# Attention with a relative bias, then a mixture of adapters: another order for the last outputs

## The chip, the core and the metric

The kernel runs on one core of one Trainium2 chip. The metric is the device time of one execution in microseconds (us). Before the change it is 201.61 us, the median of three runs (200.8 to 201.71).

A core has a matrix engine (TensorE, in the profile PE, with its weight loads as PEld), three others that compute (VectorE or DVE, ScalarE or ACT, GpSimd or POOL), and SyncE (SP), which here issues nearly all DMA transfers, among them all stores of the output. The engines run side by side, each takes its own instructions in the order of the program, and they wait for each other through semaphores. Matrix products land in PSUM, a small memory of eight banks, from which VectorE or ScalarE must copy them to SBUF before they can be stored or used as an operand.

## The reference

Two parts. The first is attention over 8 batches, 8 heads, 576 positions and 64 channels, with a bias that depends on the distance of the two positions only:

```python
    scores = scale * np.matmul(q, k.transpose(0, 1, 3, 2))
    ...
    bias = bias_table[bucket]
    scores = scores + bias.transpose(2, 0, 1)[None, :, :, :]
    scores = scores - np.max(scores, axis=-1, keepdims=True)
    attn = np.exp(scores)
    attn = attn / (np.sum(attn, axis=-1, keepdims=True) + 1e-09)
    return np.matmul(attn, v).astype(np.float32)
```

The heads of a position are then put side by side, which gives x with 4608 rows of 512. The second part picks for each row the two of eight experts with the largest logits, and adds their low-rank products (rank 16), weighted by a softmax over the two:

```python
    logits = x @ w_gate
    topk = np.argpartition(-logits, K, axis=1)[:, :K]
    ...
            z = x[mask] @ A[e]
            delta[mask] += w[mask, k, None] * (z @ B[e])
    return (x + delta).astype(np.float32)
```

## The kernel before

**Units.** One unit is a batch and a pair of heads; there are 32, U0 and U1 are the last two. The first 512 positions of a batch are its main part, the last 64 its tail. `keys` makes scores of a unit on TensorE (product, then a bias product into the same bank) and ScalarE takes their exp. `values` multiplies the exps with v, with the sums of the softmax in an extra column, and `normalise` on VectorE takes the reciprocal of the sums (L557) and multiplies (L558); the result goes to the tile `xs` of the batch. In the last two units the scores are made in halves of the queries: `keys_half(u, j, m)` makes one score tile for query half j, with its exp at L451. The values of half j need both m.

**Rows of the second part.** The output of a batch has four main tiles of 128 rows, (b, 0) to (b, 3); the tails of two batches make one tile (b, 4) with odd b. Tiles 0 and 1 need half j = 0 of all four units of the batch, tiles 2 and 3 need half 1. L is the last batch, 7. Each tile goes through these steps: x is turned (`turn` with `x_item`: transposes on TensorE, L368 and L370, and a copy from PSUM, L372), a product with A and the gate weights gives 128 low-rank values and 8 logits (`moe_z` or `zsum`), the gate is worked out (`moe_s` on GpSimd, `moe_w` with a tanh on ScalarE and the rest on GpSimd, because a softmax over two is a tanh of half the difference), the gated values zt are turned, and a last product with B gives the delta. Then x is added and the tile stored.

There are two ways to the output. `moe_d` and `out_dve` make the product with B and let VectorE add x while it leaves PSUM (L303). `out_x` adds x on TensorE, as four products of the turned x with the identity (`x_first`, L832) ahead of the product with B (L838), and the result is copied out by ScalarE or VectorE (L840). A store is one DMA of 256 KB, for a tail tile two of 128 KB (L331).

**PSUM.** Two banks rotate for values and small things (`mp`, through `bank()` at the end). The other six are three pairs that rotate for scores and for turned tiles: `score_tile` gives the next pair, and whoever asks waits until the pair's last reader is done. For the last outputs the three pairs are given back and become six single banks, `fin(i, k)`: pair i, counted from the pair whose turn it is, bank k.

**The order of the work** is the order of the program text, engine by engine. The end before: scores of U0 (1,1) and U1 (1,0); the turn of zt of (L-1,0) and (L-1,1); gating of (L-1,2) and (L-1,3); values of U1 half 0; `moe_d` of (L-1,0); scores of U1 (1,1); one turn for zt of (L-1,2), (L-1,3) and x of (L,0), (L,1); then U0 half 1 with `moe_d` of (L-1,1) ahead of it; low-rank values of (L,0), (L,1), with their gate on GpSimd; a turn for the tail tile and most of x of (L,2), (L,3). Then the values of U1 half 1 in two pieces, with the outputs of (L-1,2), (L-1,3) and products of the last tiles between them. From them comes `xl`, the last quarter of x of (L,2) and (L,3); it is turned to xb, which completes z1, the low-rank values and logits of these two tiles. Their gate is worked out straight from PSUM: the two largest by L959, their negated sum `ns`, tanh on ScalarE (`fth`, L963), the mask and the gate on VectorE, and `fzt`. The outputs follow in the order (L,0), (L,2), (L,3), (L,4), (L,1).

Of the kernel before, what the change touches and what calls it, by code (L numbers as in the profile page):

```python
# [38 lines left out]
def kernel(  # L39
# [11 lines left out]
    nc = tc.nc  # L51
# [299 lines left out]
            t.group, t.k = g, k  # L351
        return g

    def turn(items):
        n = sum(it[1] for it in items)
        assert n <= 16
        ps = score_tile("tx", (128, 2, 1024), BF16)
        sb = txp.tile([128, 16, 2, 64], BF16, name="tx", tag="tx")
        s0 = 0
        for _, k, src, quarter in items:  # L360
            for i in range(k):
                c = s0 + i
                for a in range(2):
                    rows = slice(a * 64, a * 64 + 64)
                    cols = slice(c * 64, c * 64 + 64)
                    if quarter:
                        for h in range(2):
                            nc.tensor.transpose(ps[h * 64:h * 64 + 64, a, cols], src(i, a, h), ident[rows, rows])  # L368
                    else:
                        nc.tensor.transpose(ps[:, a, cols], src(i, a), ident[rows, rows])  # L370
            s0 += k
        nc.vector.tensor_copy(sb[:, :n], ps.rearrange("p a (c i) -> p c a i", i=64)[:, :n])  # L372
        s0 = 0
        for done, k, *_ in items:
            done(sb, s0)
            s0 += k
# [17 lines left out]
    def x_item(t, g0=0, g1=HP):  # L394
        if g0 == 0:
            t.xT = [None] * HP

        def done(sb, s0):
            for hp in range(g0, g1):
                t.xT[hp] = sb[:, s0 + hp - g0].rearrange("p a i -> p (a i)")  # L400
        return done, g1 - g0, lambda i, *a: t.src(g0 + i, *a), t.quarter

    def zt_item(t):
        def done(sb, s0):
            t.zT = sb[:, s0].rearrange("p a i -> p (a i)")
        zt, k = t.group.zt, t.k
        return done, 1, lambda i, a: zt[a * 64:a * 64 + 64, k].rearrange("p e r -> p (e r)"), False
# [182 lines left out]
    def moe_w(g):  # L590
        n = g.n
        sm, mk = g.gating
        th = ms.tile([128, n, E], FP32, name="th", tag=f"th{n}")
        nc.scalar.activation(th, sm, ACT.Tanh)
        g0 = ms.tile([128, n, E], FP32, name="g0", tag=f"g0{n}")
        nc.gpsimd.tensor_tensor(g0, th, mk, op=ALU.mult)
# [3 lines left out]
        nc.gpsimd.tensor_tensor(g.zt, g.z[:, :, :ER].rearrange("p n (e r) -> p n e r", e=E),  # L600
                                gate.to_broadcast((128, n, E, r)), op=ALU.mult)
# [247 lines left out]
    def bank():  # L849
        return mp.tile([128, 512], FP32, name="fm", tag="mm")  # L850
# [31 lines left out]
    halves_of(U0, (1, 0))  # L882
    step(U0, 0, [(L - 2, 4)], z=(L - 1, 3))
    halves_of(U0, (1, 1))
    halves_of(U1, (1, 0))
    turn([zt_item(T(L - 1, 0)), zt_item(T(L - 1, 1))])
    moe_w(groups[(L - 1, 2)])

    pv = bank()
    pv_main(U1, pv, 0, KO)  # L890
# [1 line left out]
    for h in range(2):  # L892
# [5 lines left out]
                            _ap(rc, 0, [[1, 4], [0, D]]), op=ALU.mult)  # L898
    nc.vector.tensor_tensor(_ap(xs[b], hp * 320 + 256, [[HP * 320, 2], [1, D]]),
                            _ap(pv, 260, [[W1, 2], [1, D]]), _ap(rc, 4, [[1, 2], [0, D]]), op=ALU.mult)  # L900
# [12 lines left out]
    fps = [ctx.enter_context(tc.tile_pool(name=f"fin{i}_ps", bufs=1, space=bass.MemoryType.PSUM))  # L913
# [14 lines left out]
    pv_last(U1, pv, 1)  # L928
    nc.vector.reciprocal(rc[:, 6:], _ap(pv, D, [[W1, 4]]))
    xl = ms.tile([128, 2, 128], BF16, name="xl", tag="xl")  # L930
    nc.vector.tensor_tensor(xl.rearrange("p f (h d) -> p (f h) d", h=2), _ap(pv, 0, [[W1, 4], [1, D]]),
                            _ap(rc, 6, [[1, 4], [0, D]]), op=ALU.mult)
    moe_w(groups[(L, 0)])
    gx = groups[(L, 4)]
    act(gx.z[:, 0, :], zx[:, :136])
    nc.vector.max(gx.top[:, 0, :], gx.z[:, 0, ER:])
    moe_s(gx)

    def full_turn(n, ps, src, copy, tag):
        v = ps[:, :64 * n].bitcast(BF16).rearrange("p (n t) -> p n t", n=n)  # L940
# [3 lines left out]
        copy(t, v)  # L944
# [6 lines left out]
    g = groups[(L, 2)]  # L951
    n = 2
    zl = z1[:, :136 * n].rearrange("p (n e) -> p n e", n=n)
    ns = ms.tile([128, n, 1], FP32, name="fns", tag="fns")
    mk = ms.tile([128, n, E], FP32, name="fmk", tag="fmk")
    th = ms.tile([128, n, E], FP32, name="fth", tag="fth")
    gate = ms.tile([128, n, E], FP32, name="fgate", tag="fgate")
    for i in range(n):
        nc.vector.max(g.top[:, i, :], zl[:, i, ER:])  # L959
    nc.vector.scalar_tensor_tensor(out=ns, in0=g.top[:, :, 0:1], scalar=-1.0, in1=g.top[:, :, 1:2],  # L960
                                   op0=ALU.mult, op1=ALU.subtract)
    for i in range(n):
        nc.scalar.activation(th[:, i, :], zl[:, i, ER:], ACT.Tanh, scale=2.0, bias=ns[:, i, :])  # L963
    nc.vector.tensor_tensor(mk, zl[:, :, ER:], g.top[:, :, 1:2].to_broadcast((128, n, E)), op=ALU.is_ge)  # L964
    moe_w(gx)
    j0 = groups[(L, 0)]
    zt0 = full_turn(2, bank(), lambda i: j0.zt[:, i].rearrange("p e r -> p (e r)"), dve, "zt0")
    for i in range(2):
        T(L, i).zT = zt0[:, i, :]
    nc.vector.scalar_tensor_tensor(out=gate, in0=th, scalar=1.0, in1=mk, op0=ALU.add, op1=ALU.mult)  # L970
    g.zt = ms.tile([128, n, E, r], BF16, name="fzt", tag="fzt")
    nc.vector.scalar_tensor_tensor(out=g.zt, in0=zl[:, :, :ER].rearrange("p n (e r) -> p n e r", e=E),
                                   scalar=0.5, in1=gate.to_broadcast((128, n, E, r)),
                                   op0=ALU.mult, op1=ALU.mult)
    out_x(T(L, 0), fin(0, 0))
    d3 = fin(2, 1)
    x_first(T(L, 2), d3)
    d4 = fin(1, 0)
    x_first(T(L, 3), d4)
    zt1 = full_turn(2, bank(), lambda i: g.zt[:, i].rearrange("p e r -> p (e r)"), dve, "zt1")  # L980
    for i in range(2):
        T(L, 2 + i).zT = zt1[:, i, :]
    out_x(T(L, 2), d3, False)
    out_x(T(L, 3), d4, False, dve)
    zt2 = full_turn(1, bank(), lambda i: gx.zt[:, i].rearrange("p e r -> p (e r)"), dve, "zt2")
    T(L, 4).zT = zt2[:, 0, :]
    out_x(T(L, 4), fin(1, 1))
    out_dve(T(L, 1), fin(0, 1))


# [28 lines left out]
```

## Time and profile before

| what | value |
|---|---|
| runs before | 201.61, 201.71, 200.8 us |
| profiled execution | 200.68 us, its span 198.8 us |
| granted TensorE clock, mean of the span | 0.949 |
| PE busy | 178.5 us (90%) |
| ACT busy | 162.8 us (82%) |
| DVE busy | 134.8 us (68%) |
| POOL busy | 122.6 us (62%) |

The span goes from the first to the last instruction of the profiled execution. In a page the line of an engine's tenths cuts the span in 40 slices of 4.97 us; a 9 is 90% busy or more. A row of the timeline gives the start and the length in us, the engine, the line of the kernel and the operation, the tile it writes and the tiles it reads, sizes and how many were merged; in brackets the engine's idle time before it and what ended that. SPq is SyncE's queue of DMA issues: the length there is that of the issuing, merged rows include the gaps, and the transfer comes later. A row of groups gives the busy time of all of a kind in us and the mean of one in ns. A row of the table of windows gives a stretch and its length, the busy time of PE, PEld, DVE, ACT and POOL with the number of instructions, the granted TensorE clock, the busy share of the 16 DMA engines and what they moved in GB/s.

### The profile page before, as it was taken

How to read it: one execution, taken by the hardware profiler on the slowest of the kernel's cores; microseconds unless marked ns; L12 is line 12 of the kernel's file. 1: busy time of each engine (PE TensorE's matmuls, PEld its weight loads, DVE VectorE, ACT ScalarE, POOL GpSimd, SP SyncE). 2: the span in 40 equal slices, each digit the busy share in tenths (PEclk: the TensorE clock that was granted, in tenths of full speed). 3: DMA queues.
4: the chain of work that ended last, by engine and by line, in shares of the span. 5: the costliest groups of instructions: out<-in, count | busy, mean ns of one | idle time of the engine just before them, and what ended most of it. 6: DMA issues, size and time to landing. Idle time of an engine off the chain costs nothing. (4 is left out here: it accounts for less than half of the span.)

```text
span 198.8 us, 9936 instructions
## 1 busy us (share of the span) xinstructions
PE 178.5 (90%) x4262; PEld 129.4 (65%) x4262; DVE 134.8 (68%) x340; ACT 162.8 (82%) x204; POOL 122.6 (62%) x299
## 2 busy tenths in 40 slices
PE   7498998988999999999999999999999999996750
PEld 2254676666777677777777777776777777884620
DVE  6544464564577778778877687778776786797541
ACT  3457779986999899999999999999999999984230
POOL 5633556495777759495949594959494939253420
PEclk9755599999999999999999999999999999999996
DMA  5767978978889978998798878759897911123416
GB/s 135 234 167 215 292 183 212 242 173 254 244 211 261 268 190 236 297 270 219 196 288 264 203 227 274 217 169 217 233 284 230 297 69 56 62 72 93 162 73 190
DMA packets 68484, 40.65 MB, mean 204 GB/s; under 512 B 22217, under 2 KB 63705, under 8 KB 68441
## 3 DMA queue, kind: packets, MB, share of 16 engines
q1 hardware_dynamic: 67896, 39.76, 70.5%
q8 instruction: 33, 0.54, 1.2%
q10 hardware_dynamic: 544, 0.26, 0.4%
q14 instruction: 11, 0.08, 0.2%
HBM read 30.56 MB, written 9.45 MB: 201 GB/s over the span
## 5 line engine op out<-in xcount | busy, mean ns | idle before, releaser
L431 ACT ACTIVATE pk<-sc 128x1024 bf16<-128x1024 f32 x120 | 113.8, 1034 | 6.0 <-PE sc L427 6.0
L422 PE MATMUL sc<-tx 64*64 64x512 bf16 x480 | 50.7, 401 | 0.0
L518 PEld LDWEIGHTS <-pk 128*128 128x128 bf16 x1024 | 38.1, 98 | 9.1 <-issue 2.1
L427 PE MATMUL sc<-Wt,anti 64*64 64x256 bf16 (+1 forms) x480 | 43.6, 318 | 0.2
L518 PE MATMUL pv<-v,pk 128*128 128x65 bf16 x992 | 42.2, 194 | 1.2 <-DVE xn L558 0.7
L372 DVE COPY tx<-tx 128x2048 bf16<-128x2048 bf16 (+6 forms) x36 | 36.3, 1009 | 10.3 <-PE tx L370 8.3
L494 ACT ACTIVATE pt<-sc 128x1024 bf16<-128x1024 f32 x32 | 32.8, 1025 | 7.8 <-PE sc L492 6.0
L558 DVE TENSOR_TENSOR xn<-pv,rc 128x320 bf16<-128x320 f32 x62 | 30.5, 491 | 2.1
L581 POOL TENSOR_TENSOR a<-z,top 128x16 f32<-128x16 f32 (+2 forms) x16 | 3.6, 224 | 37.0 <-DVE top L571 33.5
L557 DVE RECIPROCAL rc<-pv 128x5 f32<-128x5 f32 x62 | 11.9, 192 | 20.8 <-PE pv L565 11.2
L303 DVE TENSOR_TENSOR ot<-dl,xn 128x512 f32<-128x512 f32 x26 | 17.9, 689 | 11.3 <-PE dl L614 10.8
L422 PEld LDWEIGHTS <-tx 64*64 64x64 bf16 x480 | 16.6, 108 | 10.0 <-issue 1.2
L136 POOL CAST v<-vs 128x512 bf16<-128x512 f32 x32 | 20.3, 634 | 3.6 <-DMA vs<-in_v_dram 3.1
L140 POOL CAST qn<-qs 128x512 bf16<-128x512 f32 x29 | 17.7, 612 | 5.6 <-DMA qs<-in_q_dram 5.3
L427 PEld LDWEIGHTS <-anti 64*64 64x64 bf16 x480 | 18.8, 109 | 1.1 <-issue 1.0
L140 POOL CAST kn<-ks 128x512 bf16<-128x512 f32 x29 | 17.8, 614 | 1.1 <-DMA ks<-in_k_dram 1.1
L499 POOL TENSOR_TENSOR pt<-pt,EL 128x128 bf16<-128x128 bf16 x32 | 13.8, 430 | 7.0 <-DVE EL L233 6.0
L535 PE MATMUL pv<-v,pt 128*128 128x65 bf16 x248 | 17.8, 195 | 0.0
L526 PE MATMUL pv<-vb,pt 128*128 128x130 bf16 x124 | 17.6, 225 | 0.0
L370 PEld LDWEIGHTS <-qn 64*128 64x128 bf16 x256 | 7.6, 96 | 12.5 <-issue 6.4
L535 PEld LDWEIGHTS <-pt 128*128 128x128 bf16 x256 | 14.2, 99 | 0.0
L565 PE MATMUL pv<-AW,tx 128*128 128x136 bf16 x124 | 12.5, 224 | 0.0
(141 smaller groups left out, 299.6 us busy)
## 6 DMA issues: line engine op xcount, KB each, us to landing
qs<-in_q_dram SPq DMA_DIRECT2D x32, 256.0 KB, 4.4
vs<-in_v_dram SPq DMA_DIRECT2D x64, 128.0 KB, 4.2
out_dram<-ot SPq DMA_DIRECT2D x32, 256.0 KB, 3.6
ks<-in_k_dram SPq DMA_DIRECT2D x62, 128.0 KB, 4.4
vt<-in_v_dram SPq DMA_DIRECT2D x16, 128.0 KB, 4.2
out_dram<-ot SPq DMA_DIRECT2D x8, 128.0 KB, 2.7
qkt<-in_q_dram SPq DMA_DIRECT2D x7, 128.0 KB, 4.6
qkt<-in_k_dram SPq DMA_DIRECT2D x7, 128.0 KB, 4.3
```

Of the source, the lines that this page charges most:

```text
L136: eng.tensor_copy(t[:, :, :, :D].rearrange("p c h d -> p h c d"), s)
L140: copy(t.rearrange("p c h d -> p h c d"), s)
L303: nc.vector.tensor_tensor(ot.rearrange("p (g x) -> p g x", g=HP), dl.rearrange("p (g x) -> p g x", g=HP), x[:, j, :, 2 * f:2 * f + 2, :].r ...
L372: nc.vector.tensor_copy(sb[:, :n], ps.rearrange("p a (c i) -> p c a i", i=64)[:, :n])
L422: nc.tensor.matmul(sc[prt, h, :], lhsT=kT[rows, c * 128 + f * 64:c * 128 + f * 64 + 64], rhs=qT[rows, :], start=True, stop=False, skip_gro ...
L427: nc.tensor.matmul(_ap(sc[prt, h, :], p0, [[256, 2], [128, 2], [1, n]]), lhsT=turned(h), rhs=_ap(Wt[rows, hp, :], 2 * y0 + (GP if e else 1 ...
L431: nc.scalar.activation(probs[u][0][:, c, :, :], sc, ACT.Exp, scale=scale)
L494: nc.scalar.activation(probs[u][1][:, 64:], sc.rearrange("p h x -> p (h x)"), ACT.Exp, scale=scale)
L518: nc.tensor.matmul(pv[:, o:o + W1], lhsT=pk_slice(u, c, h, j + 2 * f), rhs=vm[:, c, h, :], start=first, stop=False, skip_group_check=True)
L526: nc.tensor.matmul(_ap(pv, h * W1, [[130, 2], [1, W1]]), lhsT=probs[u][1][:, x0:x0 + 128], rhs=tvs[b % 2][:, 2 * hp + h].rearrange("p f d ...
L535: nc.tensor.matmul(pv[:, o:o + W1], lhsT=probs[u][1][:, x0:x0 + 128], rhs=vts[u % NV][:, c, h, :], start=False, stop=False, skip_group_che ...
L558: nc.vector.tensor_tensor(xs[b][:, j, hp], _ap(pv, 0, [[W1, 5], [1, D]]), _ap(rc, 6 * j, [[1, 5], [0, D]]), op=ALU.mult)
```

## The change

Only the end of the program is changed, from the scores of the last unit on.

- The last score tile, U1 (1,1), is made directly behind U1 (1,0).
- `moe_d` of (L-1,0) and (L-1,1) go from between the values to the end, and (L-1,2), (L-1,3) too. The values of U1 half 0, U0 half 1 and U1 half 1 follow each other, with only turns of x between them; the values of U1 half 1 are one piece.
- `turn` takes the copying engine as an argument. The turn of x of (L,0), (L,1) and that of the tail tile are now separate and ScalarE copies them; the zt of (L-1,2), (L-1,3) are turned in the end, by `full_turn`.
- The group (L,0), (L,1) gets the gate straight from PSUM that (L,2), (L,3) had, each with a bank and tiles of its own. The gate is split in three functions, `gate_top`, `gate_tanh` and `gate_sum`, so that the two groups interleave. The tail tile keeps its gate on GpSimd.
- All nine last outputs go by `out_x`, six copied by ScalarE and three by VectorE; for most, `x_first` is put ahead of the time at which zt is turned, in a bank of its own.

```diff
-    def turn(items):
+    def turn(items, copy=nc.vector.tensor_copy):
...
-        nc.vector.tensor_copy(sb[:, :n], ps.rearrange("p a (c i) -> p c a i", i=64)[:, :n])
+        copy(sb[:, :n], ps.rearrange("p a (c i) -> p c a i", i=64)[:, :n])
...
     halves_of(U0, (1, 1))
-    halves_of(U1, (1, 0))
+    halves_of(U1, (1, 0), (1, 1))
     turn([zt_item(T(L - 1, 0)), zt_item(T(L - 1, 1))])
-    moe_w(groups[(L - 1, 2)])
...
-    moe_d(T(L - 1, 0))
-
-    halves_of(U1, (1, 1))
-    turn([zt_item(T(L - 1, 2)), zt_item(T(L - 1, 3)), x_item(T(L, 0)), x_item(T(L, 1))])
-    step(U0, 1, [(L - 1, 1)])
-    zj = bank()
-    for i in range(2):
-        zsum(zj, i, T(L, i), range(HP), i == 0)
-    zcopy(groups[(L, 0)], zj, dve)
-    turn([x_item(T(L, 4)), x_item(T(L, 2), 0, 3), x_item(T(L, 3), 0, 3)])
...
+    step(U0, 1)
+    moe_w(groups[(L - 1, 2)])
+    turn([x_item(T(L, 0)), x_item(T(L, 1))], act)
 
     pv = bank()
-    pv_main(U1, pv, 1, (0, 2))
-    out_x(T(L - 1, 2), fin(1, 0))
-    out_x(T(L - 1, 3), fin(1, 1))
-    z1, zx = fin(2, 0), fin(2, 1)
-    zsum(zx, 0, T(L, 4), range(HP), True)
-    for i in range(2):
-        zsum(z1, i, T(L, 2 + i), range(HP - 1), i == 0)
-    pv_main(U1, pv, 1, (1, 3), False)
+    pv_main(U1, pv, 1, KO)
     pv_last(U1, pv, 1)
...
-    moe_w(groups[(L, 0)])
-    gx = groups[(L, 4)]
-    act(gx.z[:, 0, :], zx[:, :136])
-    nc.vector.max(gx.top[:, 0, :], gx.z[:, 0, ER:])
-    moe_s(gx)
+    turn([x_item(T(L, 4))], act)
+    turn([x_item(T(L, 2), 0, 3), x_item(T(L, 3), 0, 3)])
...
+    def turned_gate(zt, n, ids, copy, tag):
+        t = full_turn(n, bank(), lambda i: zt[:, i].rearrange("p e r -> p (e r)"), copy, tag)
+        for i, x in enumerate(ids):
+            T(*x).zT = t[:, i, :]
+
+    z0, z1 = fin(0, 0), fin(0, 1)
+    for i in range(2):
+        zsum(z0, i, T(L, i), range(HP), i == 0)
     xb = full_turn(2, bank(), lambda f: xl[:, f, :], dve, "xb")
+    zx = bank()
+    zsum(zx, 0, T(L, 4), range(HP), True)
+    for i in range(2):
+        zsum(z1, i, T(L, 2 + i), range(HP - 1), i == 0)
     for i in range(2):
         T(L, 2 + i).xT[HP - 1] = xb[:, i, :]
         zsum(z1, i, T(L, 2 + i), range(HP - 1, HP), False)
...
+    gx = groups[(L, 4)]
+    act(gx.z[:, 0, :], zx[:, :136])
+    nc.vector.max(gx.top[:, 0, :], gx.z[:, 0, ER:])
+    moe_s(gx)
...
+    def gate_top(i, zl):
+        w = Gate()
+        w.g, w.zl = groups[(L, i)], zl[:, :272].rearrange("p (n e) -> p n e", n=2)
+        w.ns = ms.tile([128, 2, 1], FP32, name="fns", tag=f"fns{i}")
+        w.th = ms.tile([128, 2, E], FP32, name="fth", tag=f"fth{i}")
+        for k in range(2):
+            nc.vector.max(w.g.top[:, k, :], w.zl[:, k, ER:])
+        nc.vector.scalar_tensor_tensor(out=w.ns, in0=w.g.top[:, :, 0:1], scalar=-1.0, in1=w.g.top[:, :, 1:2],
+                                       op0=ALU.mult, op1=ALU.subtract)
+        return w
+
+    def gate_tanh(w):
+        for k in range(2):
+            nc.scalar.activation(w.th[:, k, :], w.zl[:, k, ER:], ACT.Tanh, scale=2.0, bias=w.ns[:, k, :])
+
+    def gate_sum(w, i):
...
+        nc.vector.tensor_tensor(mk, w.zl[:, :, ER:], w.g.top[:, :, 1:2].to_broadcast((128, 2, E)), op=ALU.is_ge)
+        nc.vector.scalar_tensor_tensor(out=gate, in0=w.th, scalar=1.0, in1=mk, op0=ALU.add, op1=ALU.mult)
+        w.g.zt = ms.tile([128, 2, E, r], BF16, name="fzt", tag=f"fzt{i}")
+        nc.vector.scalar_tensor_tensor(out=w.g.zt, in0=w.zl[:, :, :ER].rearrange("p n (e r) -> p n e r", e=E),
+                                       scalar=0.5, in1=gate.to_broadcast((128, 2, E, r)),
+                                       op0=ALU.mult, op1=ALU.mult)
+
+    w0 = gate_top(0, z0)
+    gate_tanh(w0)
+    w1 = gate_top(2, z1)
+    gate_tanh(w1)
     moe_w(gx)
...
+    out_x(T(L - 1, 0), fin(1, 0))
+    gate_sum(w0, 0)
+    p1 = fin(1, 1)
+    x_first(T(L - 1, 1), p1)
+    d = [fin(2, 0), fin(2, 1)]
     for i in range(2):
...
+        x_first(T(L, i), d[i])
+    turned_gate(w0.g.zt, 2, ((L, 0), (L, 1)), act, "zt0")
+    gate_sum(w1, 2)
+    turned_gate(groups[(L - 1, 2)].zt, 2, ((L - 1, 2), (L - 1, 3)), act, "zta")
+    out_x(T(L - 1, 1), p1, False)
     for i in range(2):
...
+        d.append(fin(1 - i, 0))
+        x_first(T(L, 2 + i), d[-1])
+    out_x(T(L, 0), d[0], False)
+    turned_gate(gx.zt, 1, ((L, 4),), dve, "zt2")
+    turned_gate(w1.g.zt, 2, ((L, 2), (L, 3)), dve, "zt1")
+    out_x(T(L, 1), d[1], False, dve)
+    out_x(T(L - 1, 2), fin(1, 1))
+    out_x(T(L, 2), d[2], False)
+    out_x(T(L, 3), d[3], False, dve)
+    out_x(T(L, 4), fin(0, 1), True, dve)
+    out_x(T(L - 1, 3), fin(2, 0))
```

More of the change, by code (lines that the diff above doesn't have):

```diff
@@ L900 @@
                             _ap(pv, 260, [[W1, 2], [1, D]]), _ap(rc, 4, [[1, 2], [0, D]]), op=ALU.mult)
-    moe_d(T(L - 1, 0))
-    halves_of(U1, (1, 1))
-    turn([zt_item(T(L - 1, 2)), zt_item(T(L - 1, 3)), x_item(T(L, 0)), x_item(T(L, 1))])
-    step(U0, 1, [(L - 1, 1)])
-    zj = bank()
-    for i in range(2):
-        zsum(zj, i, T(L, i), range(HP), i == 0)
-    zcopy(groups[(L, 0)], zj, dve)
-    turn([x_item(T(L, 4)), x_item(T(L, 2), 0, 3), x_item(T(L, 3), 0, 3)])
+    step(U0, 1)
+    moe_w(groups[(L - 1, 2)])
+    turn([x_item(T(L, 0)), x_item(T(L, 1))], act)
+    pv = bank()
+    pv_main(U1, pv, 1, KO)
+    pv_last(U1, pv, 1)
+    nc.vector.reciprocal(rc[:, 6:], _ap(pv, D, [[W1, 4]]))
+    xl = ms.tile([128, 2, 128], BF16, name="xl", tag="xl")
+    nc.vector.tensor_tensor(xl.rearrange("p f (h d) -> p (f h) d", h=2), _ap(pv, 0, [[W1, 4], [1, D]]),
+                            _ap(rc, 6, [[1, 4], [0, D]]), op=ALU.mult)
+    turn([x_item(T(L, 4))], act)
+    turn([x_item(T(L, 2), 0, 3), x_item(T(L, 3), 0, 3)])
     s0 = next(turns)
@@ L950 @@
         zsum(z1, i, T(L, 2 + i), range(HP - 1, HP), False)
[L951 to L961, printed above, removed]
@@ L962 @@
-    for i in range(n):
-        nc.scalar.activation(th[:, i, :], zl[:, i, ER:], ACT.Tanh, scale=2.0, bias=ns[:, i, :])
-    nc.vector.tensor_tensor(mk, zl[:, :, ER:], g.top[:, :, 1:2].to_broadcast((128, n, E)), op=ALU.is_ge)
-    moe_w(gx)
-    j0 = groups[(L, 0)]
-    zt0 = full_turn(2, bank(), lambda i: j0.zt[:, i].rearrange("p e r -> p (e r)"), dve, "zt0")
-    for i in range(2):
-        T(L, i).zT = zt0[:, i, :]
-    nc.vector.scalar_tensor_tensor(out=gate, in0=th, scalar=1.0, in1=mk, op0=ALU.add, op1=ALU.mult)
@@ L971 @@
[L971 to L980, printed above, removed]
@@ L981 @@
-    for i in range(2):
[L982 to L988, printed above, removed]
+    gx = groups[(L, 4)]
+    act(gx.z[:, 0, :], zx[:, :136])
+    nc.vector.max(gx.top[:, 0, :], gx.z[:, 0, ER:])
+    moe_s(gx)
+    class Gate:
+        pass
+    def gate_top(i, zl):
[8 more added lines that the diff above has]
+        return w
@@ new lines, in gate_tanh @@
+    def gate_tanh(w):
+        for k in range(2):
+            nc.scalar.activation(w.th[:, k, :], w.zl[:, k, ER:], ACT.Tanh, scale=2.0, bias=w.ns[:, k, :])
+    def gate_sum(w, i):
+        mk = ms.tile([128, 2, E], FP32, name="fmk", tag=f"fmk{i}")
+        gate = ms.tile([128, 2, E], FP32, name="fgate", tag=f"fgate{i}")
+        nc.vector.tensor_tensor(mk, w.zl[:, :, ER:], w.g.top[:, :, 1:2].to_broadcast((128, 2, E)), op=ALU.is_ge)
[4 more added lines that the diff above has]
+                                       op0=ALU.mult, op1=ALU.mult)
```

6 lines of the change are left out of this document (removed).

## The prediction

> **What bounds the kernel now.** I read the page first. TensorE and ScalarE are both nearly full up to the last four of the 40 slices (4.97 us each), in which they empty.
>
> ```profile
> span 198.8 us, 9936 instructions
> PE   7498998988999999999999999999999999996750
> ACT  3457779986999899999999999999999999984230
> ```
>
> So the end, from about 178 us on, has no full engine and is a chain. The chain of waits (from a start of about 190 us; start, length, what) says which:
>
> ```profile
> 191.32 0.30 DVE zt L944
> 191.67 0.62 PE f L838 x2
> ...
> 193.83 0.69 DVE ot L303
> ```
>
> Turn, project, evict: one output after another, the last eviction done at 194.52. Behind it stands SyncE's queue:
>
> ```profile
> 186.39 1.08 SPq L309 DMA_DIRECT2D out_dram<-ot  x2
> 191.42 0.33 SPq L309 DMA_DIRECT2D out_dram<-ot  x1
> 192.71 0.81 SPq L309 DMA_DIRECT2D out_dram<-ot  x2
> 194.23 1.11 SPq L331 DMA_DIRECT2D out_dram<-ot  x2
> 195.43 0.54 SPq L309 DMA_DIRECT2D out_dram<-ot  x1
> ```
>
> The two halves of the tail store hold it until 195.34, so the last store starts 0.91 us after its data. Then the transfers (table of windows; the last two columns are the busy share of the DMA engines and GB/s):
>
> ```profile
> 192.20:192.90 0.70, 0.35 (x6) 0.18 (x4) 0.59 (x1) 0.48 (x1) 0.00 (x0) 1.00 0.93 351
> 194.30:194.90 0.60, 0.00 (x0) 0.00 (x0) 0.22 (x1) 0.00 (x0) 0.00 (x0) 1.00 1.02 386
> 195.40:196.20 0.80, 0.00 (x0) 0.00 (x0) 0.00 (x0) 0.00 (x0) 0.00 (x0) 0.64 0.96 213
> 196.20:197.20 1.00, 0.00 (x0) 0.00 (x0) 0.00 (x0) 0.00 (x0) 0.00 (x0) 0.50 0.95 285
> 197.20:198.00 0.80, 0.00 (x0) 0.00 (x0) 0.00 (x0) 0.00 (x0) 0.00 (x0) 0.50 0.19 69
> ```
>
> The bytes end near 197.35 (0.19 of 0.8 us), 1.45 us before the span's end. Three readings for later. A 256 KB store fills the engines for 0.70 us (first row: 351 GB/s x 0.70 us is 246 of its 262 thousand bytes). The tail pair and the last store together (524 thousand bytes) take from 195.4 to 197.35, 1.95 us. And the bytes of a store begin some 0.8 us after its issue (the output issued at 191.42 fills the first row, from 192.2).
>
> **The front of the change.** Up to the scores of half (1,0) of the last unit, at 178.31, the programs agree. These rows set what follows:
>
> ```profile
> 178.00 1.94 ACT L451 ACTIVATE pk<-sc 128x1024 bf16<-128x1024 f32 x2 [0.34 <-PE sc L447]
> 178.24 0.11 PEld L370 LDWEIGHTS <-zt 64*128 64x128 bf16 x4
> 178.41 0.67 PE L518 MATMUL fm<-v,pk 128*128 128x65 bf16 x16
> 179.54 0.20 DVE L896 RECIPROCAL frc<-fm 128x6 f32<-128x6 f32 x1
> 180.11 0.28 DVE L899 TENSOR_TENSOR xn<-fm,frc 128x128 bf16<-128x128 f32 x1
> 180.49 1.02 ACT L451 ACTIVATE pk<-sc 128x1024 bf16<-128x1024 f32 x1 [0.15 <-PE sc L447]
> 181.75 0.12 PEld L370 LDWEIGHTS <-zt 64*128 64x128 bf16 x4 [1.51 <-POOL zt L600]
> 182.17 0.75 PEld L518 LDWEIGHTS <-pk 128*128 128x128 bf16 x16
> 187.36 0.42 DVE L931 TENSOR_TENSOR xl<-fm,frc 128x256 bf16<-128x256 f32 x1
> ```
>
> *Scores at once.* The scores of (1,1) follow directly, some 0.4 us of TensorE, and their exp joins the two before it: 179.94 to about 180.96 instead of 180.49 to 181.51. The price: three score buffers rotate, and the turn of the two gated tiles now takes the buffer that the exp ending near 178.97 must free, so it goes at 179.02 instead of 178.24. TensorE works in order; the values of U1 half 0 move from 178.41 to about 179.2, their reciprocal from 179.54 to 180.32, the last normalise (L899) to 181.17. Loss on the path: 0.8 us. This wait isn't in the old trace; its bounds are 0 (buffer already free) and 2.0 us (if it waited for the newest exp, 180.96, instead).
>
> *Values ahead.* The two moe_d and the turn with its 1.51 us wait for GpSimd no longer stand ahead of U0 half 1: its values start at about 180.15 instead of 182.17; with 1.13 us of values (as from 178.41 to 179.54) and 0.7 for a reciprocal and one product (three instructions take 0.85 from 179.54 to 180.39), this half is normalised near 182.0. The gating that was waited for (moe_w) now has until 186 us. The turn of tiles (L,0) and (L,1) comes at 181.2 to 181.6, then U1 half 1 runs in one piece from 181.55, since its exp is done by 181: without the tails 0.8 of those 1.13 us. With a reciprocal of 0.2 from 182.4 and 0.42 for xl, xl ends at about 183.0 instead of 187.78: 4.8 us earlier. That is the main gain; it comes from outputs, turns and a wait taken out from ahead of it.
>
> *Turned tiles on ScalarE.* Neither copy has a row. These stand nearest:
>
> ```profile
> L840 ACT COPY ot<-f 128x512 f32<-128x512 f32 x5 | 2.8, 587 | 6.7 <-DMA out_dram<-ot 4.3 <-PE f L838 1.6 <-ACT th L594 0.8
> L473 ACT ACTIVATE pcx<-cn 128x256 bf16<-128x256 f32 x1 | 0.4, 378 | 0.0
> L372 DVE COPY tx<-tx 128x1280 bf16<-128x1280 bf16 x2 | 1.6, 816 | 1.3 <-PE tx L370 1.3
> L944 DVE COPY zt<-fm 128x256 bf16<-128x256 bf16 x2 | 0.6, 286 | 0.5 <-PE fm L942 0.5
> ```
>
> The copy for (L,0), (L,1) has 1024 elements: I take 1.02 us, the exp of that size at 180.49; below, VectorE's 0.82 for 1280 elements; above, two 512-copies, 1.17. It runs 181.7 to 182.7, that of (L,4) (512 elements, 0.59) to 183.3. ScalarE is idle there in any case. VectorE meanwhile makes xl and the third turn's copy (to about 183.55) and xb (to 183.85).
>
> **The gates.** Before, xl's end at 187.78 led to the end of fzt at 190.82, 3.04 us:
>
> ```profile
> 187.70 0.16 DVE L936 MAX8 top<-z 128x8 f32<-128x8 f32 x1
> 188.91 0.25 DVE L959 MAX8 top<-f 128x8 f32<-128x8 f32 x2 [0.46 <-PE fm L942]
> 189.44 0.43 ACT L963 ACTIVATE fth<-f,fns 128x8 f32<-128x8 f32 x2 [2.32 <-DVE fns L960]
> 189.91 0.17 DVE L964 TENSOR_TENSOR fmk<-f,top 128x16 f32<-128x16 f32 x1 [0.56 <-ACT fth L963]
> 190.12 0.21 POOL L596 TENSOR_TENSOR g<-th,mk 128x8 f32<-128x8 f32 x1 [0.95 <-ACT th L594]
> 190.40 0.42 DVE L972 SCALAR_TENSOR_TENSOR fzt<-f,fgate 128x256 bf16<-128x256 f32 x1
> 190.68 0.40 POOL L600 TENSOR_TENSOR zt<-z,gate 128x128 bf16<-128x128 f32 x1
> ```
>
> Now there are two such gates and the single one. The sums for z1 are ready near 184.3; gx's max ends there too; VectorE then does top and ns of w0 (to 184.73) and w1 (to 185.15). ScalarE does two tanh pairs (0.43 each) to 185.63 and gx's tanh to 185.85, behind which all evictions queue. VectorE, mask after tanh as in the old order, ends fzt of w0 at 185.97 and of w1 at 186.72: 4.1 us earlier than before, 3.7 us behind xl where it was 3.04. GpSimd's gating of (L,0) falls away. The single gate took 3.4 us from its max at 187.70 to the end of its zt at 191.08, 0.95 of it a wait for the tanh; I take 2.5, so from 184.3 its zt is there at 186.8.
>
> **Nine outputs at the end.** One output costs TensorE 0.44 us, start to start:
>
> ```profile
> 185.09 0.39 PE L832 MATMUL f<-ident,tx 128*128 128x128 bf16 x4
> 185.53 0.39 PE L832 MATMUL f<-ident,tx 128*128 128x128 bf16 x4
> 185.78 1.07 ACT L840 COPY ot<-f 128x512 f32<-128x512 f32 x2 [4.26 <-DMA out_dram<-ot]
> ```
>
> Nine make 4.0 us spread over six, mostly ahead of need. ScalarE evicts six (0.54 to 0.59 each, 3.4 us) and copies two turned tiles (0.38 each): 4.15 us from 185.85, plus 0.35 of waits for (L-1,2) and (L-1,3), whose banks must first be emptied and refilled. It ends at about 190.35. VectorE's zt2, zt1 and three evictions (0.69, as at 193.83) fit in 187.45 to 190.3. So the last eviction is 4.2 us earlier than 194.52.
>
> Stores are ready at 186.4, 187.75, 188.3, 188.6, 189.0, 189.55, 189.6, 190.3 (the tail, two issues) and 190.35. SyncE spaces them by 0.42 us and the tail's by 0.52 and 0.68, as in its rows above: the last is issued at about 191.65, 3.8 us earlier than 195.43.
>
> **The transfers take part of this back.** Of the nine outputs four had been issued by 187.47 (the row at 186.39), under other work; now all follow the second eviction closely. From the second store's bytes (187.8 + 0.8 = 188.6) six stores at 0.70 and the trio of 1.95 need 6.15 us: last byte 194.75 instead of 197.35, and 1.45 us of closing work give a span of 196.2. Gain 2.6 us. Without queueing, 191.65 + (197.35 - 195.43) + 1.45 = 195.0 would gain 3.8, the best end. The Trainium skill's page "DMA: Bandwidth & Descriptors" (Specifications) bounds a core's HBM traffic at about 358 GB/s; the row 194.30:194.90 shows 386, so the trace doesn't keep to it over 0.6 us. By the page the six stores would need 4.4 us instead of 4.2, and the gain would be an estimated 2.4.
>
> **The sum.** The profiled execution took 200.68 us (span 198.8 and 1.9 around it): 200.68 - 2.6 = 198.1. The median shown is 201.61, 0.93 above that execution; the runs go from 200.8 to 201.71. Against the median the forecast is 199.0.
>
> **The rivals** (times against the median).
>
> *Slow front.* If the first wait costs its upper 2.0 us instead of 0 to 0.8, or TensorE's turn of (L,0) and (L,1) waits for all earlier normalising, the second store slips by up to 2.0 us and so does the drain: gain 0.6, 201.0. For it: TensorE's order is strict and the old trace shows waits of 1.5 us at just this turn. Against it: the buffers rotate by count, so the oldest exp is the one waited for.
>
> *ScalarE too long.* Each of its ten or so links in the end may wait 0.2 us for a TensorE that is itself waiting for it; the last eviction is then near 192.5, the last issue at 193.75, the span 197.1: gain 1.7, 199.9. For it: their ready times interlock. Against it: outputs already begun with x_first need a single matmul.
>
> *Slow drain, the other side.* The last nine outputs are 2.36 million bytes. Eight of them follow 188.6, 2.10 million; the old end is reached at 2.10 million / (197.35 - 188.6) = 240 GB/s, and below it the change loses. For it: the window at 195.40 shows engines 0.96 busy moving only 213, at which 9.85 us are needed: last byte 198.45, 1.1 us later, 202.7. Against it: that window holds the half-width tail stores, and whole stores alone ran at 351 to 386.
>
> **Chances and range.** Forecast 0.62, slow front 0.11, long ScalarE 0.11, slow drain 0.16. About 0.5% (1.0 us) is what a measurement of this kernel tells from no change. Faster takes the forecast and the long ScalarE: 0.73; the slow front lies inside: 0.11; slower 0.16. The likeliest case alone spans 197.8 (no queueing in the drain) to 200.3 (half of the slow front). The range goes from 197.4 to 202.0: it holds the first three cases and leaves out the slow drain.
>
> **What would show it.** Right: exps of L451 without a gap at 179.9; xl near 183; ScalarE evictions closely spaced from about 186 and the last near 190.4; DMA share near 1 from 189 to 195. Wrong: the values of U1 half 0 later than 179.5; ScalarE idle over 1 us between its evictions; the DMA engines full at under 240 GB/s; or a last issue later than 193.

## The result, and the profile after

| | before | changed |
|---|---|---|
| median of the runs | 201.46 us (200.8 to 201.71) | 198.54 us (197.86 to 198.93) |
| ratio, 95% interval | | 0.9856 (0.982 to 0.9893) |
| profiled execution, its span | 200.68, 198.8 us | 198.93, 197.0 us |

The change makes the kernel 2.9 us faster. The forecast was 199.0 us. First the page of the changed kernel: the span, then the busy tenths of TensorE, ScalarE and the DMA engines in 40 slices of 4.9 us.

```profile
span 197.0 us, 9952 instructions
PE   7497998986999999999999999998999999999860
ACT  3459679974899999999999999998999999999670
DMA  5757978998977788978888967887879851114066
```

Before, TensorE and ScalarE thinned out over the last four slices; now over the last three, and the last two slices of DMA stand at 6. The timeline of the changed kernel, from the first score tile that the old order also had:

```profile
179.43 2.85 ACT L451 ACTIVATE pk<-sc 128x1024 bf16<-128x1024 f32 x3 [0.34 <-PE sc L447]
180.51 0.23 PE L370 MATMUL tx<-ident,zt 64*128 64x64 bf16 x4 [0.39 <-ACT pk L451]
180.68 0.67 PE L518 MATMUL fm<-v,pk 128*128 128x65 bf16 x16
181.57 0.56 PEld L518 LDWEIGHTS <-pk 128*128 128x128 bf16 x16
181.80 0.20 DVE L895 RECIPROCAL frc<-fm 128x6 f32<-128x6 f32 x1 [0.73 <-PE fm L537]
182.91 1.56 ACT L372 COPY tx<-tx 128x1024 bf16<-128x1024 bf16 x2 [0.52 <-PE tx L370]
183.84 0.42 DVE L910 TENSOR_TENSOR xl<-fm,frc 128x256 bf16<-128x256 f32 x1
...
187.62 0.42 DVE L977 SCALAR_TENSOR_TENSOR fzt<-f,fgate 128x256 bf16<-128x256 f32 x1
```

The exp of U0 (1,1) starts at 179.43 here, and at 178.00 in the execution of before. Up to it the two programs are the same, so these 1.43 us belong to the executions and not to the change. Everything below is therefore measured from the start of this exp, in each trace. **The stretch** is what lies between it and the end of the span: 20.8 us before, 17.6 us now, 3.2 us less. (Spans are given to 0.1 us.) In this clock xl ended at 9.78 before and ends at 4.83 now.

The evictions on ScalarE and the issues on SyncE of the changed kernel:

```profile
186.81 0.58 ACT L840 COPY ot<-f 128x512 f32<-128x512 f32 x1
188.21 1.09 ACT L840 COPY ot<-f 128x512 f32<-128x512 f32 x2
189.50 1.07 ACT L840 COPY ot<-f 128x512 f32<-128x512 f32 x2 [0.20 <-PE f L838]
190.85 0.59 ACT L840 COPY ot<-f 128x512 f32<-128x512 f32 x1 [0.28 <-ACT ot L840]
```

```profile
187.42 4.51 SPq L309 DMA_DIRECT2D out_dram<-ot  x7
192.02 1.28 SPq L331 DMA_DIRECT2D out_dram<-ot  x2
193.40 0.54 SPq L309 DMA_DIRECT2D out_dram<-ot  x1
```

And its table of windows (columns as before; the last two are the busy share of the DMA engines and GB/s):

```profile
188.00:189.00 1.00, 1.00 (x16) 0.75 (x14) 0.32 (x3) 1.00 (x4) 0.03 (x1) 1.00 0.70 262
189.00:190.00 1.00, 1.00 (x13) 0.69 (x11) 0.81 (x3) 0.80 (x3) 0.00 (x0) 1.00 0.32 119
190.00:191.00 1.00, 0.77 (x9) 0.32 (x5) 1.00 (x2) 0.72 (x3) 0.00 (x0) 1.00 1.03 385
191.00:192.00 1.00, 0.00 (x0) 0.00 (x0) 0.22 (x1) 0.44 (x1) 0.00 (x0) 1.00 1.02 379
192.00:193.00 1.00, 0.00 (x0) 0.00 (x0) 0.00 (x0) 0.00 (x0) 0.00 (x0) 1.00 1.02 381
193.00:194.00 1.00, 0.00 (x0) 0.00 (x0) 0.00 (x0) 0.00 (x0) 0.00 (x0) 0.96 1.05 350
194.00:195.00 1.00, 0.00 (x0) 0.00 (x0) 0.00 (x0) 0.00 (x0) 0.00 (x0) 0.50 0.97 291
195.00:195.50 0.50, 0.00 (x0) 0.00 (x0) 0.00 (x0) 0.00 (x0) 0.00 (x0) 0.50 0.98 377
```

The last eviction ends at 191.44, 12.0 us after the exp; before it was 16.5. So the computing became 4.5 us shorter, the stretch only 3.2. In between stand the transfers: from 190 on the DMA engines are full to 195.5, four microseconds after the last engine has stopped. The last store is issued 1.96 us behind its data.

The ratios in the next section are those of fast runs, and one profiled execution there, that of four stores left out, was a slow one (198.05 us, where the fast runs of that kernel took 194.96 to 196.39); counted from the exp, its steps up to the eviction of (L,0) agree with the changed kernel to 0.01 us.

### The profile page after: what moved, and what is told of

It reads as the page before. It is cut to its first block, busy times and chain, and to the rows that moved or that the text cites. A ratio compares the mean times of both kernels' runs of the same rounds, so it can differ in the third digit from the quotient of the medians.

```text
span 197.0 us, 9952 instructions
## 1 busy us (share of the span) xinstructions
PE 178.4 (91%) x4272; PEld 130.2 (66%) x4272; DVE 134.6 (68%) x340; ACT 165.6 (84%) x210; POOL 120.9 (61%) x292
## 4 chain that ended last, share of the span: by engine, by line
PE 52%; ACT 18%; DMA 10%; issue 6%; DVE 5%; SPq 4%; POOL 1%; POOLq 0%; ACTq 0%
ACT pk L431 14%; PE pv L518 11%; PE tx L370 8%; PE sc L422 6%; PE sc L427 4%; PE sc L492 3%; PE sc L489 3%; ACT pt L494 3%; DMA Bf<-in_moe_B_dram 3%; DMA qkt<-in_k_dram 3%; PE pv L535 2%; PE pv L526 2%; PE pv L565 2%; PE dl L614 2%; DMA vs<-in_v_dram 2%
## 5 line engine op out<-in xcount | busy, mean ns | idle before, releaser
L372 DVE COPY tx<-tx 128x2048 bf16<-128x2048 bf16 (+7 forms) x35 | 35.2, 1007 | 9.4 <-PE tx L370 7.4
L303 DVE TENSOR_TENSOR ot<-dl,xn 128x512 f32<-128x512 f32 x24 | 16.6, 690 | 11.0 <-PE dl L614 11.0
L422 PEld LDWEIGHTS <-tx 64*64 64x64 bf16 x480 | 16.1, 108 | 10.2 <-issue 1.6
L140 POOL CAST kn<-ks 128x512 bf16<-128x512 f32 x29 | 17.8, 613 | 0.8 <-DMA ks<-in_k_dram 0.8
L535 PE MATMUL pv<-v,pt 128*128 128x65 bf16 x248 | 17.8, 195 | 0.0
L526 PE MATMUL pv<-vb,pt 128*128 128x130 bf16 x124 | 17.6, 225 | 0.0
L504 DVE TENSOR_TENSOR pt<-pt,ET 128x256 bf16<-128x256 bf16 x32 | 12.5, 394 | 0.1
```

What stands on the lines that cost most here:

```text
L140: copy(t.rearrange("p c h d -> p h c d"), s)
L422: nc.tensor.matmul(sc[prt, h, :], lhsT=kT[rows, c * 128 + f * 64:c * 128 + f * 64 + 64], rhs=qT[rows, :], start=True, stop=False, skip_gro ...
L526: nc.tensor.matmul(_ap(pv, h * W1, [[130, 2], [1, W1]]), lhsT=probs[u][1][:, x0:x0 + 128], rhs=tvs[b % 2][:, 2 * hp + h].rearrange("p f d ...
L535: nc.tensor.matmul(pv[:, o:o + W1], lhsT=probs[u][1][:, x0:x0 + 128], rhs=vts[u % NV][:, c, h, :], start=False, stop=False, skip_group_che ...
```

## The experiments

Two questions: which parts of the change carry the 4.5 us, and what takes 1.3 of them back. Each kernel is the changed one with the edit shown. The table gives, from the profiled execution of each and counted from the start of the exp of U0 (1,1): the end of xl, the end of the eviction of (L,0), the end of the span (the stretch), and what lies between the last two. The ratio is that of the times to the kernel before on the same chip, with its interval.

| kernel | xl | (L,0) evicted | stretch | rest | ratio |
|---|---|---|---|---|---|
| changed | 4.83 | 9.87 | 17.6 | 7.7 | 0.9856 (0.982 to 0.9893) |
| changed, second time | 4.82 | 9.86 | 17.6 | 7.8 | 0.9787 (0.9724 to 0.9851) |
| scores late | 4.60 | 9.63 | 17.4 | 7.8 | 0.983 (0.9752 to 0.9909) |
| copies on VectorE | 5.00 | 10.01 | 17.8 | 7.8 | 0.9803 (0.9755 to 0.9851) |
| last store by ScalarE's queue | 4.83 | 9.86 | 17.5 | 7.6 | 0.9829 (0.9761 to 0.9897) |
| four stores left out | 4.83 | 9.86 | 16.0 | 6.2 | 0.9729 (0.9675 to 0.9783) |
| two outputs between the values | 6.52 | 11.38 | 18.9 | 7.6 | 0.9872 (0.9798 to 0.9945) |
| two outputs early | 4.82 | 11.42 | 19.0 | 7.6 | 0.9965 (0.9923 to 1.0007) |
| gate on GpSimd | 4.83 | 11.35 | 19.1 | 7.8 | 0.996 (0.991 to 1.001) |
| second store early | 4.82 | 9.77 | 17.4 | 7.6 | 0.9801 (0.9718 to 0.9885) |
| second store early, scores late | 4.59 | 9.53 | 17.1 | 7.6 | 0.9826 (0.9761 to 0.9892) |
| tail from two queues | 4.83 | 9.87 | 18.0 | 8.1 | 0.9853 (0.9785 to 0.992) |
| the last three together | 4.59 | 9.54 | 17.8 | 8.3 | 0.9833 (0.977 to 0.9896) |

The intervals of the ratios are 0.7 to 1.7% wide. The times tell the two rows at 0.996 from the changed kernel, and four stores left out from its first measurement, but none of the others. The intervals of the two rows at 0.996 even take in 1, though their stretch is 1.7 to 1.8 us under the 20.8 of before. The stretch tells more: two executions of the changed kernel agree to 0.1 us.

**Scores late.**

```diff
-    halves_of(U1, (1, 0), (1, 1))
+    halves_of(U1, (1, 0))
...
+    halves_of(U1, (1, 1))
     step(U0, 1)
```

> The changed kernel with one part undone: the scores of U1 (1,1) are made behind the values of U1 half 0 again. Measure: the stretch from the start of the exp of U0 (1,1) (line 451) to the end of the span, 20.8 us before the change and 17.6 us after it. Theory (the gain lies in the order of the values; scores at once buy little, because they push the turn of the zt back by 0.8 us): the turn of the zt goes 0.8 us earlier, the exp of (1,1) about 1.7 us later, xl within 0.3 us of where it is, stretch 17.3 to 17.9 us, time within 0.2% of the changed kernel. Rival (the early exp is what lets the values follow each other): U1 half 1 waits for its exp, stretch 18.4 us or more.

The stretch is 17.4 us and xl comes 0.23 us earlier, as the theory had it. The early exp isn't what lets the values follow each other; made at once, the scores cost a little.

**Copies on VectorE.** All four turned tiles that ScalarE copies are copied by VectorE:

```diff
-    turn([x_item(T(L, 0)), x_item(T(L, 1))], act)
+    turn([x_item(T(L, 0)), x_item(T(L, 1))])
...
-    turn([x_item(T(L, 4))], act)
+    turn([x_item(T(L, 4))])
```

and in the same way `zt0` and `zta`.

> The changed kernel with all turned tiles copied by VectorE. Theory (the copies on ScalarE cost nothing because it is idle there, and VectorE is the nearer engine of the chain): VectorE gets 0.7 us ahead of xl and 0.4 us behind it, xl ends 0.3 to 0.7 us later, the sums of z1 0.6 to 1.0 us later; the first eviction follows, the last stores queue a little less; stretch 17.9 to 18.4 us. Rival (the transfers alone set the end): stretch unchanged within 0.2 us. Second rival (ScalarE is the bound of the end, 0.75 us of copies fewer on it): 0.3 to 0.7 us shorter.

The stretch is 17.8, 0.2 us more: the sign of the theory, at the foot of its range. xl is only 0.17 us later, since VectorE had gaps too. ScalarE's copies are worth 0.2 us.

**Last store by ScalarE's queue.** The product and copy of `out_x` for (L-1,3) are unchanged; its store is issued with `t.store(ot, nc.scalar)`.

> The changed kernel with its last store, (L-1,3), issued by ScalarE's DMA queue in place of SyncE's, where it stands 1.96 us behind its data (ready 191.44, issued 193.40). Theory (the DMA engines are full from 190 to 195.5, the queue of issues is only where it shows): the store is issued 1.9 us earlier, the bytes end at the same time, stretch 17.6 us within 0.3. Rival (the issuing on SyncE, 0.5 to 0.7 us each, is the bound): stretch shorter by 1.2 to 1.9 us.

The issue and the DMA engines in this kernel (a row of the timeline, then windows):

```profile
191.74 0.37 ACTq L309 DMA_DIRECT2D out_dram<-ot  x1
```

```profile
193.00:194.00 1.00, 0.00 (x0) 0.00 (x0) 0.00 (x0) 0.00 (x0) 0.00 (x0) 0.57 1.03 387
194.00:195.00 1.00, 0.00 (x0) 0.00 (x0) 0.00 (x0) 0.00 (x0) 0.00 (x0) 0.50 1.05 344
195.00:196.00 1.00, 0.00 (x0) 0.00 (x0) 0.00 (x0) 0.00 (x0) 0.00 (x0) 0.50 0.71 207
```

Its exp starts at 179.70, so the issue at 12.04 is 1.93 us earlier than in the changed kernel (13.97). The stretch stays at 17.5. The engines are as full as before and end as late. SyncE's long queue is where the wait shows, not where it comes from.

**Four stores left out.** `out_x` gets a flag, and (L-1,0) to (L-1,3) aren't stored.

> The changed kernel without the four stores of the tiles (L-1,0) to (L-1,3): these rows are computed and evicted but not written. 1.05 of the last 2.36 million bytes are gone. Theory (the transfers take back more than 1 us of the gain): the DMA engines are no longer full throughout, the last store is the tail pair, ready at 191.2 and issued then, last byte near 193.2, stretch 15.0 to 15.7 us. Rival (the chain of gates and evictions sets the end, transfers lie under it): only the last eviction falls away, stretch 17.0 to 17.5 us.

```profile
190.00:191.00 1.00, 1.00 (x10) 0.61 (x8) 0.81 (x2) 0.80 (x3) 0.00 (x0) 1.00 0.01 2
191.00:192.00 1.00, 0.61 (x6) 0.27 (x4) 1.00 (x2) 0.71 (x2) 0.00 (x0) 1.00 1.00 373
...
193.00:194.00 1.00, 0.00 (x0) 0.00 (x0) 0.00 (x0) 0.00 (x0) 0.00 (x0) 1.00 1.04 350
194.00:195.00 1.00, 0.00 (x0) 0.00 (x0) 0.00 (x0) 0.00 (x0) 0.00 (x0) 0.84 0.71 199
```

The stretch is 16.0 us: between the theory's range and the rival's. Windows of this kernel (exp at 180.28) show why: the engines do nothing until the bytes of (L,0) come at 191.0, 10.7 us after the exp, and are then full to 194.7. Even five tiles, ready within 2 us of each other, are a queue. So the leftover stores take 1.6 us at the end, and the end is a drain without them too. Nearly all of it, 1.5 us, is in the rest behind (L,0) (6.2 instead of 7.7): only two of the four stores, (L-1,2) and (L-1,3), stand there, each 0.70 us of the engines by the reading of the old trace.

**Two outputs between the values.**

```diff
-    step(U0, 1)
+    moe_d(T(L - 1, 0))
+    step(U0, 1, [(L - 1, 1)])
```

and `out_x` of these two tiles is taken out of the end.

> The changed kernel with one part undone: the outputs of (L-1,0) and (L-1,1) stand between the values again, by line 303, as before the change. Stretch from the exp of U0 (1,1) to the end: 17.6 us changed, 20.8 before. Theory (outputs between the values delay the chain by what they take of TensorE and VectorE, 0.2 and 0.7 us each, but their bytes leave the full DMA stretch at the end, which begins only with the gated outputs): xl 0.9 to 1.6 us later, the rest of the chain with it, 0.5 to 0.8 us of ScalarE's evictions fewer, five plus two tiles in the drain; stretch 17.4 to 18.4 us. Rival (having the values ahead of all outputs is the whole gain): stretch 18.8 us or more.

Rows of its timeline (exp at 177.66):

```profile
180.79 1.28 DVE L303 TENSOR_TENSOR ot<-dl,xn 128x512 f32<-128x512 f32 x2
```

```profile
180.93 0.10 PEld L614 LDWEIGHTS <-tx 128*128 128x128 bf16 x1 [1.04 <-DVE xn L898]
180.94 0.10 PEld L518 LDWEIGHTS <-pk 128*128 128x128 bf16 x1
181.53 0.53 PEld L518 LDWEIGHTS <-pk 128*128 128x128 bf16 x15 [0.49 <-issue]
```

```profile
181.53 0.65 PE L518 MATMUL pv<-v,pk 128*128 128x65 bf16 x16 [0.20 <-DVE ot L303]
```

The stretch is 18.9: the rival's number. The second output needs one of the two rotating banks, which VectorE frees at the end of L898: 1.04 us of waiting. The values of U0 half 1 then need the other, which L303 holds. They start at 3.87 instead of 2.14 us after the exp, xl is 1.69 us late, (L,0) 1.5, the end 1.4. What two outputs save behind xl is 0.3 us, because their bytes go out ahead of those of (L,0) in any case. This is how the two outputs cost when they follow each other; in the old order they stood further apart, and its trace has a shorter wait for a bank:

```profile
183.74 0.63 PE L856 MATMUL fm<-AW,tx 128*128 128x136 bf16 x8 [0.43 <-DVE ot L303]
```

**Gate on GpSimd.** The group (L,0), (L,1) goes back to `zcopy`, `moe_s` and `moe_w`:

```diff
-    w0 = gate_top(0, z0)
-    gate_tanh(w0)
+    j0 = groups[(L, 0)]
+    zcopy(j0, z0, dve)
...
+    moe_w(j0)
     moe_w(gx)
...
-    gate_sum(w0, 0)
```

> The changed kernel with the gate of the group (L,0), (L,1) worked out on GpSimd again, behind that of the single tail tile, instead of straight from PSUM. Theory (the gate of (L,0) sets when the drain becomes continuous): the turned gate comes 0.9 to 1.6 us later, and the stretch follows, 18.4 to 19.2 us. Rival (evictions on ScalarE and the drain have room for it): within 0.3 us of 17.6.

```profile
188.42 0.62 POOL L600 TENSOR_TENSOR zt<-z,gate 128x256 bf16<-128x256 f32 x1
```

```profile
189.42 0.37 ACT L928 COPY zt<-fm 128x256 bf16<-128x256 bf16 x1 [1.17 <-PE fm L926]
189.69 0.38 ACT L928 COPY zta<-fm 128x256 bf16<-128x256 bf16 x1
189.95 1.10 ACT L840 COPY ot<-f 128x512 f32<-128x512 f32 x2
```

Its exp starts at 179.70. The turned gate is copied at 9.72 instead of 8.24 us after it, (L,0) is evicted 1.5 us later, and the stretch is 1.5 us longer, as the theory had it: all of the gate's delay reaches the end.

**Two outputs early.** Both are put ahead of the last two sums of z1:

```diff
+    out_x(T(L - 1, 0), fin(1, 0))
+    out_x(T(L - 1, 1), fin(1, 1))
     for i in range(2):
         T(L, 2 + i).xT[HP - 1] = xb[:, i, :]
```

and they are taken out of their places in the end.

> The changed kernel with the outputs of (L-1,0) and (L-1,1) made and evicted just ahead of the last two sums of z1, where ScalarE has gaps. Measure: the stretch from the exp of U0 (1,1) to the end, 17.6 us. Theory, from the runs so far (the end of the eviction of (L,0) plus 7.5 us of drain: changed 9.9 + 7.7, tile (L-1,1) early 9.8 + 7.6, two outputs between the values 11.4 + 7.6): TensorE is full up to the sums, so the two outputs cost the gates 0.9 us, ScalarE saves part of it behind them, (L,0) is evicted 0.3 to 0.7 us later, and the earlier first bytes buy nothing because the same seven tiles follow: stretch 17.7 to 18.2 us. Rival (the nine stores are one queue, and starting it 1 us earlier ends it earlier): 16.6 to 17.2 us.

Rows of ScalarE, one of VectorE and windows of this kernel (exp at 179.52):

```profile
186.00 1.07 ACT L840 COPY ot<-f 128x512 f32<-128x512 f32 x2 [1.44 <-PE f L832]
186.96 0.29 ACT L951 COPY z<-fm 128x136 f32<-128x136 f32 x1
```

```profile
187.28 0.17 DVE L952 MAX8 top<-z 128x8 f32<-128x8 f32 x1 [2.06 <-ACT z L951]
```

```profile
188.00:189.00 1.00, 0.00 (x0) 0.00 (x0) 0.84 (x4) 0.77 (x5) 0.45 (x3) 1.00 0.85 318
189.00:190.00 1.00, 0.81 (x13) 0.74 (x13) 0.80 (x4) 0.49 (x2) 0.81 (x3) 1.00 0.00 0
190.00:191.00 1.00, 1.00 (x12) 0.75 (x12) 0.58 (x3) 0.74 (x2) 0.00 (x0) 1.00 0.00 0
```

19.0 us, worse than the theory and against the rival. The two stores do begin earlier, and then the engines stand still for over two microseconds until (L,0) comes. The last sums of z1 end 0.9 us later, as the theory booked (6.96 instead of 6.08 us after the exp). The rest of the delay comes from ScalarE's order, which it didn't book: z of the single gate, ready early, stands behind both evictions, which wait for TensorE (1.44 us); VectorE waits for z 2.06 us with both other gates behind it. (L,0) is 1.55 us late.

**Second store early, alone and with scores late.** The output of (L-1,1) goes directly behind that of (L-1,0), ahead of `gate_sum(w0, 0)` and of the turned gates.

> The changed kernel with the output of (L-1,1) directly behind that of (L-1,0), ahead of the turned gates. In the changed kernel the DMA engines stand still from 188.9 to 189.7 between the first and the second store, and are full from 190 to 195.5. Theory (the drain sets the end, so filling its one gap pays, though ScalarE turns the gates 0.3 us later): second store ready 0.8 us earlier, (L,0) 0.2 to 0.4 us later, stretch 16.9 to 17.4 us against 17.6. Rival (the gates set the end): stretch 17.6 to 18.0 us.

> The changed kernel with the scores of U1 (1,1) behind the values of U1 half 0 and the output of (L-1,1) directly behind (L-1,0). Alone these gave stretches of 17.4 and 17.4 us against 17.6. Theory (one moves the chain, the other fills a gap of the drain): the two add, 17.0 to 17.3 us, time 0.1 to 0.3% under the changed kernel. Rival (both act on the same slack): 17.3 to 17.5 us.

17.4 alone and 17.1 with the scores late: the two add, 0.5 us below the changed kernel. In the first, half of the 0.2 us is (L,0), which is evicted 0.1 us earlier where the theory had it 0.2 to 0.4 us later. The other half is in the rest, 7.6 instead of 7.7 to 7.8: the bytes of the second store no longer go out directly ahead of those of (L,0). Each half is near the rounding of the spans. The second version has the shortest stretch of those that store everything, but in time (0.9826, interval to 0.9892) it can't be told from the changed kernel (0.9787 beside it).

**The changed kernel again.**

> The changed kernel as it is, beside the others on the same chip. Both theories: stretch 17.4 to 17.8 us, ratio to the kernel before 0.980 to 0.990; it gives the others their level.

17.6 us, as the first time. The ratio, 0.9787, lies just outside the expected range; the first was 0.9856, and their intervals overlap. That is how far a ratio of a few runs goes here.

**Tail from two queues, and all together.** (L-1,3) is moved ahead of (L,4), whose store becomes `t.store(ot, (nc.sync, nc.scalar))`.

> The changed kernel with the tail tile stored last, its two halves of 64 rows at the same time from the queues of SyncE and ScalarE. In the changed kernel the DMA engines are as full at 194.0 to 194.5 as before it, but move 217 GB/s where they moved 380: there the halves go one after the other. Theory (a half of 64 partitions alone is read at about half the rate, and two halves side by side are not): the dip goes, 0.4 to 0.6 us; stretch 16.9 to 17.3 us. Rival (each of the tail's packets is slow by itself): same dip, stretch 17.4 to 17.8 us.

> The changed kernel with three things together: scores of U1 (1,1) behind the values of U1 half 0 (17.4 us of stretch alone), the output of (L-1,1) directly behind (L-1,0), and the tail stored last from two queues. Theory (the drain sets the end, the three act on its start, its gap and its rate): the gains add, stretch 16.3 to 16.9 us, time 0.3 to 0.6% under the changed kernel. Rival (gates and evictions set the end): 17.4 us or more.

Rows of the first (exp at 179.13): the two issues, then windows.

```profile
191.28 0.54 ACTq L331 DMA_DIRECT2D out_dram<-ot  x1
```

```profile
192.39 1.32 SPq L331 DMA_DIRECT2D out_dram<-ot  x1
```

```profile
193.50:194.00 0.50, 0.00 (x0) 0.00 (x0) 0.00 (x0) 0.00 (x0) 0.00 (x0) 1.00 1.15 246
194.00:194.50 0.50, 0.00 (x0) 0.00 (x0) 0.00 (x0) 0.00 (x0) 0.00 (x0) 0.61 0.84 193
```

18.0 and 17.8 us: 0.4 longer than without, and 0.7 longer than the version with the two other edits. The first is above both the theory and the rival; the second lies where the rival put it. The dip of the rate is still there. The halves didn't go side by side, though: SyncE's was issued 1.1 us after ScalarE's, behind full queues, and its issuing took 1.32 us. Whether halves at the same moment would run at the full rate stays open.

Undone one at a time, the values ahead of the outputs give back 1.4 us of the stretch, the gate straight from PSUM 1.5, the copies on ScalarE 0.2 and the scores at once -0.2: together 2.9 of the 3.2. They were not undone together, so whether they add is not shown.

## Why the prediction was right

Point by point, in microseconds from the start of the exp of U0 (1,1); the prediction's times are taken from its 178.00.

| step | predicted | measured |
|---|---|---|
| turn of zt, held by the score buffer | 1.02 | 1.08 |
| values of U1 half 0 | 1.2 | 1.25 |
| values of U0 half 1 | 2.15 | 2.14 |
| xl ends | 5.0 | 4.83 |
| second fzt ends | 8.72 | 8.61 |
| first eviction begins | 7.85 | 7.38 |
| last eviction ends | 12.35 | 12.01 |
| last store issued | 13.65 | 13.97 |
| last byte | 16.75 | 16.1 |
| stretch | 18.2 | 17.6 |

The order of the forecast holds: values ahead of outputs, gates sooner, evictions closely spaced, then a drain that takes part of the gain back. The gain was put at 2.6 us; the stretch lost 3.2, the medians 2.9. Three sizes were off. ScalarE's first eviction came 0.5 us sooner than worked out, and the drain became continuous 0.4 us sooner. The tail pair and the last store were given 1.95 us, as in the old trace, and took about 1.65 (the drain runs from 10.2 to 16.05, less six stores at 0.70): the dip of the rate is there (291 GB/s from 194 to 195), but in windows of a quarter of a microsecond the rate is under 300 GB/s for 0.75 us, where before it was for 1.5. And SyncE's issues were 0.3 us later than worked out, at no cost.

That the time came so close is in part luck. The executions differ ahead of the exp by more than the forecast was off, and the second comparison, 0.9787, would make it 197.3 us from 201.61, just under the range given.

Of the reasons, the drain is shown: issuing the last store 1.9 us earlier changes nothing, leaving four stores out takes 1.6 us away. What the prediction didn't see is how exactly it works: in all ten executions that store nine outputs with the tail from SyncE's queue alone, the span ends 7.6 to 7.8 us after (L,0) leaves PSUM, whatever goes before. It is 7.6 in the four that evict (L-1,1) well ahead of (L,0), and 7.7 to 7.8 in the others but the one with the last store by ScalarE's queue (7.6). That is the seven tiles from (L,0) on, queued in front of the DMA engines. So the end is set by when the first gated output is there, and a delay of it comes through in full (1.5 us with the gate on GpSimd). For the gain ahead of xl the prediction named outputs, turns and a wait taken out; the experiment with two outputs between the values shows 1.4 us of the 3.2 there, in that kernel by a mechanism it didn't name, the two rotating PSUM banks, for which TensorE waits until VectorE has normalised or added x. In the old order that wait was 0.43 us, and the longer one there is the one that the prediction named, the turn's 1.51 us for GpSimd. The loss of 0.8 us booked for the scores at once is real at its place; undone, it gives back only 0.2 us, because the scores then stand among the values.

The slow front didn't come: the buffer waited for was the one counted. Nor did a ScalarE too long: its waits between evictions are 0.2 and 0.28 us. The slow drain, with 0.16 the main danger, didn't come either: from 190 to 193 the engines moved 379 to 385 GB/s, well over the 240 at which the gain would be gone. The bound of about 358 GB/s that the Trainium skill's page "DMA: Bandwidth & Descriptors" (Specifications) gives doesn't agree with these windows, now over three microseconds.

xl gained 4.95 us, of which the two outputs give back 1.69. What the turn's wait for GpSimd, the leftover outputs of (L-1,2) and (L-1,3) and the two pieces of U1 half 1 cost before was not tried by itself, so how the other 3.3 us divide is not shown.

## What to carry to other kernels

When a kernel ends in several stores, look for the moment from which the DMA engines are full to the end. Here what brought the first store of that queue earlier paid in full, and a second issuing queue and earlier stores ahead of a gap paid little or nothing. An output put between the steps of a chain costs, beside its instructions, the PSUM banks and the places in an in-order engine's queue that it takes. Where an unchanged beginning differs by more than the change is worth, count from a common instruction near the edit instead of from the start.

## What was not expected of the hardware

- The program ahead of the exp of U0 (1,1) is the same in all kernels here, and this exp started between 176.24 (second store early) and 180.28 us (four stores left out) after the start. That is 4 us of difference between executions, more than the whole change. The mean granted clock doesn't explain it: it was 0.963 in the early one and 0.979 in the late one.
- Where the tail's stores of 64 partitions go out, the rate drops though the engines stay busy. In the changed kernel, by a finer window than above, it is 217 GB/s, against 385 from 190 to 191 with stores of 128 partitions; the same dip is in every kernel here.

```profile
194.00:194.50 0.50, 0.00 (x0) 0.00 (x0) 0.00 (x0) 0.00 (x0) 0.00 (x0) 0.50 0.93 217
```

- Issuing took longer deep in the drain. In the changed kernel the first store took SyncE 0.34 us and the last 0.54. The store of a half took 0.47 us with one store issued 1.1 us before it (the first of the pair in the old end), and 1.32 us in the kernel with two queues, behind eight stores in 5.2 us. What made it longer was not tried by itself.
